# Keeping every softmax sum, testing their extremes at the end, and a second path on the chip for sums out of range

## The chip, the cores and the metric

The kernel runs on one core of one Trainium2 chip. The metric is the device time of one execution in microseconds (us). Before the change it is 411.09 us, the median of 3 runs (410.84 to 411.49).

The core has a matrix engine (PE, with its weight loads shown apart as PEld), three engines for elementwise work (DVE, ACT and POOL) and one that mostly issues transfers (SP). Each runs its own list of instructions in order, and they wait for each other through semaphores.

## The reference: what is computed

Two parts follow each other: a convolution whose seven taps have softmax weights of their own at every position and head, and a two-layer network with a maximum in the middle. Cut to what matters:

```python
# x: (8, 4160, 192), weight_gen: (8, 4160, 8 heads, 7 taps), w1 and w2: (192, 1024), w_out: (1024, 192), all float32
w = np.exp(weight_gen - np.max(weight_gen, axis=-1, keepdims=True))
w = w / (np.sum(w, axis=-1, keepdims=True) + 1e-09)
x_pad = concatenate([zeros((8, 6, 192)), x], axis=1)             # six rows of zeros ahead of each sequence
out = einsum('bshk,bskhg->bshg', w, x_unf)                        # x_unf[b, s, k] = x_pad[b, s + k], 8 heads of 24
h1, h2 = out @ w1, out @ w2
return np.maximum(h1, h2) @ w_out                                 # (33280, 192)
```

weight_gen is drawn with a standard deviation of 0.3 and x with 0.1.

## The kernel before

**The layout.** The 33,280 positions are dealt out to the 128 partitions: partition p holds 260 consecutive ones, called its columns. Columns go through in 17 batches, sixteen of 16 and one of 4; the batches are cut into units of 4 or 8 columns.

**The softmax without its maximum.** The kernel never subtracts the maximum. For a batch b, `exp_sum` (L135, ACT) takes the exponential of the loaded weights `wg_t` into `e_t`; `red` (L147, DVE) sums it over the seven taps into `sum_t`, a tile from a pool of three buffers; `ln` (L151, ACT) replaces the sum by its logarithm in place; `shift` (L156, DVE) subtracts that logarithm from the weights; and `weights` (L167, ACT) takes the exponential once more, now normalised, each value written twice in bfloat16 into `en_t`. This holds as long as the sums neither overflow nor vanish.

**The convolution and the network.** `mul` (L182, DVE) multiplies the taps into `m_t`, `adds` (L198, L204, L207, DVE) adds them up into `y_t`, and a transfer transposes the result into `yt` (L216, issued by SP; in the first two batches PE sums and transposes instead, L248). PE then forms h2 - h1 with the difference of the two weight matrices (`hid_tile`, L299), ACT takes its positive part (`relu`, L309) into `rd_t`, and PE adds `rd_t @ w_out` to `yt` times the product of w1 and w_out (`out_first`, L351, and `out_hidden`, L339). `evac` (L395, ACT) copies the result to `o_t`, and SP issues its store (L409). The last two columns have a tile of their own, `o_last` (copy L383); ACT and SP store one of them each (L386).

**The order** is written out by hand. Work is recorded in the order of the loop at the end (L785 to L800), engine by engine. `softmax_steps` and `extra` place the steps of later batches beside the matrix products of earlier groups of tiles, by the table `AT` and the dictionary `due`. After the last group, `rest_of_results` (L800) computes and stores the last results in three parts, and nothing but PE, ACT and the stores is left.

**The end.** The program closes with code that the framework puts in (recorded as L825, as L814 at the start): SP waits in turn for the semaphore of every transfer queue, then all engines meet in a barrier, POOL clears the semaphores, and they meet again.

Of the kernel before, what the change touches and what calls it, by code (L numbers as in the profile page):

```python
# [9 lines left out]
FP32 = mybir.dt.float32  # L10
BF16 = mybir.dt.bfloat16
# [6 lines left out]
def _sub(base: bass.AP, off: int, dims):  # L18
    ap = [list(base.ap[0])] + [[int(s), int(c)] for s, c in dims]
    return dataclasses.replace(base, offset=base.offset + off, ap=ap)  # L20
# [3 lines left out]
def kernel(  # L24
# [18 lines left out]
    HF = F // 2  # L43
    CPP = B * S // P
    RPB = P // B
    G = D // H
    assert RPB * CPP == S

# [24 lines left out]

    ctx.enter_context(tc.manual_schedule())
    consts = ctx.enter_context(tc.tile_pool(name="consts", bufs=1))
    pwg = ctx.enter_context(tc.tile_pool(name="pwg", bufs=4))
    pxb = ctx.enter_context(tc.tile_pool(name="pxb", bufs=2))
    pe_ = ctx.enter_context(tc.tile_pool(name="pe", bufs=2))
    psm = ctx.enter_context(tc.tile_pool(name="psm", bufs=3))
    pm = ctx.enter_context(tc.tile_pool(name="pm", bufs=1))  # L80
    pen = ctx.enter_context(tc.tile_pool(name="pen", bufs=2))
    py = ctx.enter_context(tc.tile_pool(name="py", bufs=2))
    pyt = ctx.enter_context(tc.tile_pool(name="pyt", bufs=6))
    prd = ctx.enter_context(tc.tile_pool(name="prd", bufs=7))
    first_ps = ctx.enter_context(ExitStack())
    ps = {k: first_ps.enter_context(tc.tile_pool(name="pps_" + k, bufs=2, space=bass.MemoryType.PSUM))
          for k in ("h", "o")}

    def later_ps():

        first_ps.close()
        for k in ("ab", "c", "r"):
            ps[k] = ctx.enter_context(tc.tile_pool(name="pps_" + k, bufs=1, space=bass.MemoryType.PSUM))

    wg_ts, xb_ts, e_ts, s_ts, en_ts, y_ts, yt_ts = {}, {}, {}, {}, {}, {}, {}

    m_t = pm.tile([P, K * 16 * D], BF16, name="m_t")

# [36 lines left out]
    def part(b, i, of):  # L137

        n = BATCHES[b][1]
        h0, h1 = n * i // of * H, n * (i + 1) // of * H  # L140
        return slice(h0, h1), h0 * K, [[K, h1 - h0], [1, K]]

    def red(b, i=0, of=1):
        if i == 0:
            s_ts[b] = psm.tile([P, BATCHES[b][1] * H], FP32, name="sum_t", tag="sum")
        hs, at, ap = part(b, i, of)
        nc.vector.reduce_sum(out=s_ts[b][:, hs], in_=_sub(e_ts[b], at, ap), axis=AX.X)  # L147

    def ln(b, i=0, of=1):
        s_t = s_ts[b][:, part(b, i, of)[0]]  # L150
        nc.scalar.activation(out=s_t, in_=s_t, func=AF.Ln)  # L151

    def shift(b, i=0, of=1):
        hs, at, ap = part(b, i, of)
        w_t = _sub(wg_ts[b], at, ap)
        nc.vector.tensor_tensor(out=w_t, in0=w_t, in1=_sub(s_ts[b], hs.start, [[1, hs.stop - hs.start], [0, K]]),  # L156
                                op=ALU.subtract)

    def weights(b, o):
# [293 lines left out]
    def out_room(now, tag=None):  # L453
        tag = tag or ("r" if "r" in ps else "o")
        w, name = {"ab": (2048, "ab"), "c": (1024, "c")}.get(tag, (1024, "op"))
        tile_ = ps[tag].tile([P, w], FP32, name="op_ps", tag=name)
        for c in now:
            op_at[c // 2] = tile_, (c - now[0]) // 2 * D
# [30 lines left out]
    def rest_of_results(c):  # L489

        parts = [p for p in (c[:4], c[4:-2], c[-2:]) if p]
        assert max(map(len, parts)) <= 4
        go = []
        for i, now in enumerate(parts):
            out_room(now, ("r", "ab", "c")[i])
            go.append(relay(out_first(now)))
            if i:
                out_second(parts[i - 1], go[i - 1])
                evac(parts[i - 1][0] // 2, len(parts[i - 1]) // 2)
        out_second(parts[-1], go[-1])  # L500
        evac(parts[-1][0] // 2, len(parts[-1]) // 2)
# [7 lines left out]
    msk_i = consts.tile([P, 1], I32, name="msk_i")  # L509
    msk = consts.tile([P, 1], FP32, name="msk")  # L510
    gate = consts.tile([P, 1], FP32, name="gate")
    o_last = consts.tile([P, 2 * D], FP32, name="o_last")

    with tc.tile_pool(name="pstage", bufs=1) as pstage:
# [179 lines left out]
        sum_transpose(3)  # L694
        weights(1, 8)

    pout = ctx.enter_context(tc.tile_pool(name="pout", bufs=1))
    o_t.append(pout.tile([P, 24 * D], FP32, name="o_t", tag="o"))


# [77 lines left out]
    def steps(g, tiles):  # L778

        if tiles:  # L780
            softmax_steps(g)
        for t in tiles:
            extra(t)

    out_room(OUTS[3])  # L785
    go = relay(out_first(OUTS[3]))
    out_second(OUTS[3], go)
# [2 lines left out]
    for g in range(4, len(GROUPS)):  # L790
        if GROUPS[g][1] == 3 and "c" not in ps:
            later_ps()
        tiles = [t for t in range(GROUPS[g][0], sum(GROUPS[g])) if t >= 16]
        if g in early:
            hidden(g, OUTS[g], early[g][0], ahead=lambda: {4: lambda: (weights(1, 12), ln(2)), }.get(g, none)())
            early[g][1]()
            steps(g, tiles)
        else:
            hidden(g, OUTS[g], beside=lambda: steps(g, tiles))
    rest_of_results(OUTS[-1])  # L800

# [1 line left out]
_INS = ['x', 'weight_gen', 'moe_w1', 'moe_w2', 'moe_w_out']  # L803
# [26 lines left out]
```

## Time and profile before

| what | value |
|---|---|
| median of 3 runs | 411.09 us (410.84 to 411.49) |
| the profiled execution: its own time | 411.11 us |
| the profiled execution: span, first to last instruction | 409.2 us |
| granted clock of PE | 1.000 |
| idle of ACT before L309, ended by PE | 26.2 us |
| DVE: reduces of the sums, L147 | 31 instructions, 19.6 us |
| ACT: logarithms of 128x128, L151 | 15 instructions, 5.0 us |
| SP: stores of o_t after 380 us, when issued | 384.20, 397.39, 399.93, 404.03, 405.27 us |
| the two stores of o_last, issue to landing | 1.8 us (SP) and 2.0 us (ACT) |

How to read it: the busy rows give each engine's busy time, its share of the span and its number of instructions; the slices cut the span in 40 equal parts, a digit for the busy share in tenths. A chain of work that ended last is followed back from the end: an engine with a large share of it sets the time. In a group of instructions the columns are line, engine, operation, output and input tile with their shapes and the count, then busy us and mean ns of one, then the idle time ahead of them and what ended it. "SPq" and "POOLq" are the sequencers of these engines: issues of transfers, waits and semaphore steps, which do not count as busy.

### The profile page before, as it was taken

The numbers are of one execution on the slowest core, as the hardware profiler recorded it, in microseconds if no ns is written. First come the engines' busy times: TensorE is split into PE (matmuls) and PEld (weight loads), VectorE is DVE, ScalarE is ACT, GpSimd is POOL, SyncE is SP. The second block draws the span as 40 slices with busy tenths as digits, with TensorE's granted clock in tenths as the row PEclk, the third lists the DMA queues.
The fourth block names the chain that finished last, engine by engine and source line by source line (L and its number), as shares of the span: only waits on it lengthen the run. The fifth ranks groups of instructions, "written<-read, shape, count | busy, mean of one in ns | idle before, by whom it ended". The sixth has DMA issues, their size and how long they took to land.

```text
span 409.2 us, 16135 instructions
## 1 busy us (share of the span) xinstructions
PE 399.1 (98%) x7422; PEld 317.7 (78%) x7422; DVE 371.9 (91%) x216; ACT 356.9 (87%) x424; POOL 74.3 (18%) x101
## 2 busy tenths in 40 slices
PE   7899899999999999999999999999999999999996
PEld 2589899777777877777787778777777877787796
DVE  5999999999999999899999999999999999999100
ACT  6799799999899998899998999998999888988872
POOL 0311120122222112122012222121122121210000
PEclk9999999999999999999999999999999999999999
DMA  8957657856658664964796496378649838743704
GB/s 239 228 128 214 115 155 161 184 144 165 148 113 243 155 155 108 239 151 96 151 249 157 94 263 172 76 230 210 122 91 258 168 51 221 186 88 89 205 34 163
DMA packets 60785, 65.70 MB, mean 161 GB/s; under 512 B 47631, under 2 KB 49039, under 8 KB 60718
## 3 DMA queue, kind: packets, MB, share of 16 engines
q1 hardware_dynamic: 52334, 40.54, 35.6%
q0 software_dynamic: 8240, 24.04, 29.6%
q8 instruction: 58, 0.95, 0.9%
q10 hardware_dynamic: 144, 0.10, 0.1%
q14 instruction: 9, 0.07, 0.1%
HBM read 35.96 MB, written 25.56 MB: 150 GB/s over the span
## 4 chain that ended last, share of the span: by engine, by line
PE 70%; DVE 18%; ACT 6%; DMA 3%; issue 2%; SPq 1%; DVEq 0%; ACTq 0%
PE op_ps L339 32%; PE hd L299 29%; DVE m_t L182 8%; PE op_ps L351 6%; DVE m_t L198 4%; DVE m_t L204 3%; ACT rd_t L309 3%; DMA ws1T<-in_moe_w_dram 2%; PE hdp L299 1%; PE yps L248 1%; DMA yt<-y_t 1%; DVE y_t L207 1%; DVE wg_t L156 1%; DVE sum_t L147 1%; ACT yt L255 1%
## 5 line engine op out<-in xcount | busy, mean ns | idle before, releaser
L309 ACT ACTIVATE rd_t<-hd 128x1024 bf16<-128x1024 f32 (+1 forms) x206 | 234.3, 1188 | 27.6 <-PE hd L299 26.2
L339 PE MATMUL op_ps<-wo,rd_t 64*128 64x192 bf16 x4160 | 211.7, 243 | 0.3 <-issue 0.2
L339 PEld LDWEIGHTS <-rd_t 64*128 64x128 bf16 x4160 | 181.8, 94 | 16.0 <-issue 0.4
L299 PE MATMUL hd<-yt,wd 64*128 64x512 bf16 (+1 forms) x1584 | 188.3, 360 | 0.4 <-DMA yt<-y_t 0.2
L182 DVE TENSOR_TENSOR m_t<-xb_t,en_t 128x10752 bf16<-128x10752 bf16 (+1 forms) x37 | 187.5, 5071 | 0.2
L299 PEld LDWEIGHTS <-wd 64*128 64x128 bf16 x1776 | 94.5, 94 | 42.4 <-issue 2.0
L224 POOL CAST gate<-yt 128x1 f32<-128x1 bf16 x29 | 39.4, 1358 | 270.0 <-DMA yt<-y_t 270.0
L198 DVE TENSOR_TENSOR m_t<-m_t 128x4608 bf16<-128x4608 bf16 (+1 forms) x30 | 74.1, 2471 | 0.1
L395 ACT COPY o_t<-op_ps 128x384 f32<-128x384 f32 (+1 forms) x99 | 57.2, 588 | 13.1 <-PE op_ps L339 13.1
L351 PE MATMUL op_ps<-w,yt 64*128 64x192 bf16 x780 | 56.0, 243 | 0.1
L351 PEld LDWEIGHTS <-yt 64*128 64x128 bf16 x780 | 38.7, 94 | 16.3 <-issue 0.9
L204 DVE TENSOR_TENSOR m_t<-m_t 128x3072 bf16<-128x3072 bf16 (+1 forms) x29 | 50.0, 1724 | 0.1
L167 ACT ACTIVATE en_t<-wg_t 128x896 bf16<-128x896 f32 (+2 forms) x45 | 35.8, 821 | 0.0
L207 DVE TENSOR_TENSOR y_t<-m_t 128x1536 bf16<-128x1536 bf16 (+1 forms) x29 | 27.3, 941 | 0.5
L156 DVE TENSOR_TENSOR wg_t<-wg_t,sum_t 128x280 f32<-128x280 f32 (+5 forms) x46 | 22.1, 482 | 2.3 <-ACT sum_t L151 2.3
L114 POOL DMA_DIRECT2D xb_t<-in_x_dram x33 | 17.6, 534 | 27.3 <-ACT rd_t L309 15.5
L147 DVE TENSOR_REDUCE sum_t<-e_t 128x64 f32<-128x448 f32 (+2 forms) x31 | 19.6, 636 | 2.8 <-ACT e_t L135 2.8
L135 ACT ACTIVATE e_t<-wg_t 128x896 f32<-128x896 f32 (+2 forms) x18 | 16.1, 900 | 2.8 <-DMA wg_t<-in_weight_gen_dram 2.8
L309 ACT ACTIVATE rd_t<-hdp 128x1024 bf16<-128x1024 f32 x16 | 16.2, 1054 | 0.4 <-PE hdp L299 0.4
L248 PE MATMUL yps<-ident,m_t 64*128 64x64 bf16 x636 | 11.0, 191 | 2.6 <-DVE m_t L182 1.6
L299 PE MATMUL hdp<-yt,wd 64*128 64x256 bf16 x192 | 13.1, 270 | 0.2
L248 PEld LDWEIGHTS <-m_t 64*128 64x128 bf16 x636 | 10.2, 95 | 3.9 <-DVE m_t L182 2.7
(45 smaller groups left out, 65.8 us busy)
## 6 DMA issues: line engine op xcount, KB each, us to landing
out_dram<-o_t SPq DMA_DIRECT2D x27, 768.0 KB, 4.7
xb_t<-in_x_dram POOLq DMA_DIRECT2D x30, 384.0 KB, 5.1
wg_t<-in_weight_gen_dram POOLq DMA_DIRECT2D x14, 448.0 KB, 5.5
xb_t<-xb_t POOLq DMA_DIRECT2D x16, 288.0 KB, 5.4
out_dram<-o_t SPq DMA_DIRECT2D x10, 384.0 KB, 2.9
wg_t<-in_weight_gen_dram SPq DMA_DIRECT2D x2, 448.0 KB, 4.6
xs<-in_x_dram SPq DMA_DIRECT2D x2, 384.0 KB, 6.7
xb_t<-in_x_dram POOLq DMA_DIRECT2D x3, 192.0 KB, 4.6
```

The source lines that it names most:

```text
L156: nc.vector.tensor_tensor(out=w_t, in0=w_t, in1=_sub(s_ts[b], hs.start, [[1, hs.stop - hs.start], [0, K]]), op=ALU.subtract)
L167: nc.scalar.activation(out=_sub(en_ts[b], (o * WGC + j * N * K) * 2, [[2 * N, K], [2, N], [1, 2]]), in_=_sub(wg_ts[b], (o * H + j * N) * K ...
L182: return nc.vector.tensor_tensor(out=m_out, in0=x_in, in1=_sub(en_ts[b], o * WGC * 2, [[2, K * n * H], [0, G // 2], [1, 2]]), op=ALU.mult,)
L198: nc.vector.tensor_tensor(out=taps(0, 1, 3), in0=taps(0, 1, 3), in1=taps(3, 1, 3), op=ALU.add)
L204: nc.vector.tensor_tensor(out=taps(0, 2, 2), in0=taps(0, 2, 2), in1=taps(1, 5, 2), op=ALU.add)
L207: nc.vector.tensor_tensor(out=_sub(y_ts[b], o * D, [[64, 2], [P, 3 * w // 2], [1, 64]]), in0=taps(0, 1, 1), in1=taps(2, 1, 1), op=ALU.add,)
L224: nc.gpsimd.tensor_copy(out=gate, in_=yt[:, 0:1])
L299: nc.tensor.matmul(hid_out(t, f, j), lhsT=wd_at(j, s, f // 4, f % 4 * P, P), rhs=_sub(yt_ts[u][half(j), :], (s + j) % 3 * P, [[3 * P, w // ...
L309: relu_of[t0] = nc.scalar.activation(out=rd[:, k * 1024:(k + n) * 1024], in_=hd[:, at:at + n * 1024], func=AF.Relu)
L339: return nc.tensor.matmul(op_out(c), lhsT=rd[half(r), k * 1024 + at:k * 1024 + at + P], rhs=wo[half(r), f * D:(f + 1) * D], start=False, s ...
L351: nc.tensor.matmul(op_out(c + j), lhsT=yt_ts[u][half(j), (3 * i + (s + j) % 3) * P:(3 * i + (s + j) % 3 + 1) * P], rhs=w10[half(j), s * D: ...
L395: nc.scalar.copy(out=_sub(o, c % 24 * D, [[D, len(qs)], [h * D, 2], [1, D]]), in_=_sub(tile_, at + (qs[0] - p) * D, [[D, len(qs)], [512, 2 ...
```

## The change

Four things are done.

1. The sums of the exponentials are no longer overwritten. `red` writes them into one of two tiles that live to the end, `sums[0]` (384 columns wide, for the first three batches) and `sums[1]` (1696 wide, for the rest); `ln` writes its logarithm into a tile `ln_t` from the pool that held `sum_t`, and `shift` reads that.
2. After the loop and ahead of `rest_of_results`, `out_of_range` is recorded: DVE takes the largest and the smallest of each of the two tiles per partition, compares them with 1e18 and 1e-18, and takes the maximum of the four answers. SP issues a transfer that turns the 128 answers, one per partition, into a row, and DVE takes its maximum as an integer `flag`, 0 or 1.
3. After `rest_of_results` all pools but `consts` are closed, every engine loads `flag` into a register and branches on it.
4. Where it is 1, `all_again` computes every column anew, one at a time in a loop of the chip, with the maximum subtracted, and overwrites all results. Where it is 0, the engines jump over it. On the path not taken the framework puts steps that bring the semaphores to where the second path would have left them: on SP eight, each a wait for a transfer queue's semaphore and an addition to it, and one each on PE, ACT and DVE. SP's closing waits are twelve in place of ten. SP's list also has four more register moves ahead of the first barrier.

```diff
+    S_MOST, S_LEAST = 1e18, 1e-18
...
-    wg_ts, xb_ts, e_ts, s_ts, en_ts, y_ts, yt_ts = {}, {}, {}, {}, {}, {}, {}
+    wg_ts, xb_ts, e_ts, l_ts, en_ts, y_ts, yt_ts = {}, {}, {}, {}, {}, {}, {}
+
+    sums = [consts.tile([P, 3 * 16 * H], FP32, name="sums")]
...
+    def s_of(b, hs):
+        c0 = BATCHES[b][0] * H - (b > 2) * 3 * 16 * H
+        return sums[b > 2][:, c0 + hs.start:c0 + hs.stop]
+
     def red(b, i=0, of=1):
-        if i == 0:
-            s_ts[b] = psm.tile([P, BATCHES[b][1] * H], FP32, name="sum_t", tag="sum")
         hs, at, ap = part(b, i, of)
-        nc.vector.reduce_sum(out=s_ts[b][:, hs], in_=_sub(e_ts[b], at, ap), axis=AX.X)
+        nc.vector.reduce_sum(out=s_of(b, hs), in_=_sub(e_ts[b], at, ap), axis=AX.X)
 
     def ln(b, i=0, of=1):
-        s_t = s_ts[b][:, part(b, i, of)[0]]
-        nc.scalar.activation(out=s_t, in_=s_t, func=AF.Ln)
+        if i == 0:
+            l_ts[b] = psm.tile([P, BATCHES[b][1] * H], FP32, name="ln_t", tag="ln")
+        hs = part(b, i, of)[0]
+        nc.scalar.activation(out=l_ts[b][:, hs], in_=s_of(b, hs), func=AF.Ln)
...
+    sums.append(pout.tile([P, (CPP - 3 * 16) * H], FP32, name="later_sums", tag="sums"))
...
+    def out_of_range():
+
+        for i, (op, beyond, limit) in enumerate(((ALU.max, ALU.is_gt, S_MOST), (ALU.min, ALU.is_lt, S_LEAST))):
+            for j in range(2):
+                nc.vector.tensor_reduce(out=ends[:, 2 * i + j:2 * i + j + 1], in_=sums[j], axis=AX.X, op=op)
+            nc.vector.tensor_single_scalar(out=ends[:, 2 * i:2 * i + 2], in_=ends[:, 2 * i:2 * i + 2],
+                                           scalar=limit, op=beyond)
+        nc.vector.tensor_reduce(out=bad, in_=ends, axis=AX.X, op=ALU.max)
+        nc.sync.dma_start(out=bad_row, in_=bad)
+        nc.vector.tensor_reduce(out=flag, in_=bad_row, axis=AX.X, op=ALU.max)
+
+    def all_again(pg, pgp):
...
+        for c0, c1 in ((0, PAD), (PAD, CPP)):
+            with tc.For_i(c0, c1) as c:
+                xw = pg.tile([P, K * D], FP32, name="g_xw", tag="g_xw")
+                nc.sync.dma_start(out=xw, in_=xe[:, bass.ds(c * D, K * D)] if c0 == 0
+                                  else x_rows[:, bass.ds(c - PAD, K), :])
+                a_column(xw, c)
...
+    out_of_range()
     rest_of_results(OUTS[-1])
+    fast.close()
+    any_bad = nc.values_load(flag[0:1, 0:1], min_val=0, max_val=1,
+                             skip_runtime_bounds_check_because="a maximum of comparisons, each 0 or 1")
+    with tc.If(any_bad > 0):
+        with tc.tile_pool(name="pg", bufs=1) as pg, tc.tile_pool(
+                name="pgp", bufs=1, space=bass.MemoryType.PSUM) as pgp:
+            all_again(pg, pgp)
```

In `all_again`, `a_column` loads one column's weights and x, computes its softmax with the maximum, multiplies and adds the taps on DVE, transposes on PE, runs the network and stores the column. The two tiles of sums shift the tiles that are allocated behind them to higher addresses.

## The prediction

> **What bounds the kernel now.** I read the span and clock of the core first (409.2 us, clock 1.000: nothing was throttled), then the page's busy rows and slices, then the chain of work that ended last, and then, because the change puts its new work at the end, the last 30 us one view at a time.
>
> ```profile
> PE 399.1 (98%) x7422; PEld 317.7 (78%) x7422; DVE 371.9 (91%) x216; ACT 356.9 (87%) x424; POOL 74.3 (18%) x101
> DVE   5999999999999999899999999999999999999100
> PE 70%; DVE 18%; ACT 6%; DMA 3%; issue 2%; SPq 1%; DVEq 0%; ACTq 0%
> ```
>
> PE is busy for 98% and carries 70% of the chain; DVE has 18% of it, all before the last three slices, where DVE stands idle. So work on DVE is dear up to about 380 us and free after it. The table of stretches says it sharply (columns: length, then PE, PEld, DVE, ACT and POOL with their counts, clock, DMA share, GB/s):
>
> ```profile
> 385.00:400.00 15.00, 15.00 (x314) 13.73 (x311) 0.00 (x0) 11.58 (x13) 0.00 (x0) 1.00 0.27 105
> 400.00:406.30 6.30, 5.34 (x130) 5.11 (x124) 0.00 (x0) 1.75 (x3) 0.00 (x0) 1.00 0.39 140
> 406.30:409.20 2.90, 0.00 (x0) 0.00 (x0) 0.00 (x0) 0.00 (x0) 0.00 (x0) 1.00 0.40 126
> ```
>
> The last 2.9 us hold no computing: only the last stores' landing and SP's closing waits. From the timelines, SP's waits and the records of L825 (the closing code):
>
> ```profile
> 379.49 0.56 DVE L207 TENSOR_TENSOR y_t<-m_t 128x768 bf16<-128x768 bf16 x1
> 405.88 0.34 SPq L386 DMA_DIRECT2D out_dram<-o_last  x1
> 405.89 0.37 ACTq L386 DMA_DIRECT2D out_dram<-o_last  x1
> SPq L825 <- DMA out_dram<-o_last: 0.6, 1, 0.6
> L825 SPq EVENT_SEMAPHORE  x7: 28/28/28, 407.9 to 408.3; - x7
> L825 POOLq EVENT_SEMAPHORE  x2: 17/17/17, 408.4 to 408.5; - x2
> ```
>
> The reader is to see the order of the end: DVE's last work ends at 380.05; the last two stores are issued until 406.22 (SP) and 406.26 (ACT); SP then waits for their landing until 407.92; from there to 408.34 it runs seven satisfied waits, one after the other, 0.42 / 7 = 61 ns each; then come the barriers, and the span ends at 409.2. POOL's two records are a wait that also takes from a semaphore and a plain add; narrowing the window puts them at 408.44 and 408.53, so a step that updates a semaphore costs about 80 ns.
>
> **What changes, step by step.** Read engine by engine, the two built programs have the same instructions with the same waits up to the end of DVE's, PE's and POOL's work, up to a semaphore's name on ACT, and on SP up to the store at 399.93. PE, ACT and DVE thus keep their order over 380 us. The durations below are of the profiled execution: 411.11 us, 1.9 more than its span, and 0.02 above the median of the three runs (411.09), so what I add to the one holds for the other.
>
> *Kept sums, Ln into a tile of its own.* 31 reduces (L147) and 18 logarithms (L151) keep their shapes; none is added. The tiles behind move up in memory by some KB. I take nothing: the multiplies of one form (L182, 128x10752) run in 5751 to 5756 ns on both turns of their buffers, so addresses do not show. Bounds: 0 to 0.1 us either way.
>
> *The test on DVE.* Two maxima and two minima over 384 and 1696 columns, two comparisons and one small maximum. From the reduces of before,
>
> ```profile
> L147 DVE TENSOR_REDUCE sum_t<-e_t 128x64 f32<-128x448 f32 x26 | 15.9, 613 | 2.8 <-ACT e_t L135 2.8
> L147 DVE TENSOR_REDUCE sum_t<-e_t 128x128 f32<-128x896 f32 x3 | 3.2, 1082 | 0.0
> ```
>
> 448 more elements cost 469 ns, 1.05 ns each, with 144 ns fixed: 0.55 us for 384, 1.92 for 1696, together 2 x 2.47 = 4.9, and three small ones at 0.15 (L560) = 0.5. From 380.05 DVE is done at 385.4. It is beside PE and ACT, and its first reader is SP's DMA, which stands behind the store of 399.93: 14.9 us of cover. Were the cover gone, it would cost 5.4.
>
> *The DMA of one number per partition into a row, and its maximum.* SP issues it at 400.33, for some 0.4 (as its neighbours). Behind it on SP stands the store at 404.03: 3.3 us to spare. It lands after 1.8 us (o_last) to 5.4 (the slowest of the last five o_t stores, 2.0/3.0/5.4), so at 402.1 to 405.7; DVE's maximum (0.15) gives the flag by 402.3 to 405.9, ahead of SP's and ACT's first need for it at 406.22 and 406.26. Cost 0.
>
> *The load of the flag and the branch, on each engine.* DVE and POOL do it as soon as the flag is there, PE after 405.35, ACT and SP after 406.22. On SP and ACT it lies beside the landing, which ends at 407.92: 1.66 us of cover. The trace has no register load. Its ends are 17 ns (an SP semaphore record) and 1.8 us (a whole store of 96 KB, issue to landing); one word out of SBUF is a round trip, but a shorter one than that store's, so I take 1.0, nearer to the upper row. The branch: SP's gap from its last issue (406.22) to the first closing record (406.27) holds a branch already and is 0.05. 406.22 + 1.0 + 0.05 = 407.3, covered. [...]
>
> *What SP does on the path not taken.* Here is the cost that nothing hides. The not-taken path raises eight DMA semaphores by what the second path would have raised them, each raise waiting for its own DMAs; SP's closing waits are twelve instead of ten, and all of them come behind the raises. Before, seven records stood behind the last landing. Now there are six raises (the first two pass while the landing runs), a branch, and twelve waits: 6 x 0.08 + 0.05 + 12 x 0.061 = 1.26, against 7 x 0.061 = 0.43. The barriers behind are unchanged. **Sum: +0.83 us, 411.11 + 0.83 = 411.9.** Bounds of this step: raises and waits at 0.05 (the spacing of SP's first two closing records, 53 ns) give 0.95 - 0.43 = +0.5; all at 0.08, with 0.1 of branch, +1.1.
>
> *At the start* SP sets four registers more before the first barrier. Its first record is at 0.00 and POOL's constants hold that barrier to 0.5, so four at 0.06 are hidden.
>
> **Rivals.**
>
> 1. *The closing steps are cheap* (not slower). All of it hangs on the mean price of a step: 18 new and old steps and the branch must exceed 0.43 + 0.82, so the side is decided at (1.25 - 0.05) / 18 = 67 ns a step. For cheap: SP's own records stand 53 and 61 ns apart. Against: none of those updates a semaphore, and POOL's that do stand 80 apart. At 53 ns: +0.5, 411.6, within 0.2%.
>
> 2. *The load outlasts the landing.* It decides from 1.6 us on. For: five engines fetch the same word, and a round trip through memory takes 1.8 here. Against: it is one word. At 1.8 to 2.2 SP enters the path at 408.1 to 408.5, with all eight raises ahead: 8 x 0.08 + 0.05 + 0.73 = 1.42, drain at 409.5 to 409.9 against 408.34: +1.2 to +1.6, **412.3 to 412.7**.
>
> 3. *The jump leaves the fetched code.*
>
> ```profile
> q8 instruction: 58, 0.95, 0.9%
> q14 instruction: 9, 0.07, 0.1%
> ```
>
> (queue, packets, MB, share of 16 engines.) 0.95 MB over PE's 14,844 instructions is 64 bytes each, in packets of 16 KB (256 instructions); the other engines share 9 of 8 KB (about 120). The second path lies between the branch and its target: 209 instructions on PE, 99 on SP, 91 on DVE, 66 on ACT, 52 on POOL. Each is under a packet, so the target is in the packet being run or in the next one. PE runs through its 58 packets with 0.3 us of idle time before L339 in all, so the next one is fetched ahead. That speaks against a stall. If jumps did refetch: 0.1% of 16 x 409.2 us over 9 is 0.7 us a packet, and 1.8 for the round trip, 2.5; SP then enters at 409.8, and with 1.42 behind drains at 411.2: +2.9, **413 to 414.5**. [...]
>
> 4. *The change does not do what it says*, and the second path runs: sums of seven exponentials of inputs of deviation 0.3 lie near 7, far from 1e18 and 1e-18. Under 1 in 100; it would add 260 columns, one after the other, behind the end.
>
> **How the numbers follow.** A difference under 0.2% (0.82 us) can't be told from none here, and my sum lies on that bound. Forecast, 411.6 to 412.2: 55%, of it 30 above the bound (411.91) and 25 below. Rival 1: 13%, below. Rival 2: 17%, above. Rival 3 with 4: 12%, above. Faster, by a luckier landing of the last stores: 3%. Slower 30 + 17 + 12 = 59%, same 25 + 13 = 38%, faster 3%. The range, 411.4 to 412.9, takes in forecast and rivals 1 and 2 (85%) and leaves out rival 3 and the gain.
>
> **What would show it.** Right: the spans from 0 to 405.9 us agree to 0.1; DVE's test ends before 387; the DMA of the row lands before 405.9; SP's raises begin before 407.9; from the last landing to SP's drain 1.1 to 1.4 us instead of 0.43. Wrong: a load of over 1.6 us, or a hole between the branch and the first raise, with a new packet in the instruction queues; or the stores of 404.03 and after later than before.

## The result, and the profile after

The changed kernel takes 414.02 us (median of 7 runs, 412.42 to 415.40) against 411.09 for the kernel before beside it (7 runs, 410.14 to 412.31): a ratio of 1.0074, 95% interval 1.0056 to 1.0092. That is +3 us where +0.8 was forecast, outside the range. The profiled execution took 413.74 us, span 411.9, clock 0.999; before, 411.11 and 409.2. Verdicts below are ratios to the kernel before, run on the same chip (its medians there: 410.9, 411.29, 410.71 and 410.73 us in the four sets). They leave out executions more than 1.5% above the fastest of their kernel, which were found in e8 alone. The lines of the changed kernel shown here count 8 higher than before, and the closing code is L926 instead of L825.

The timeline of the changed kernel at its end (start, length, engine, line; in brackets the idle time before and what ended it):

```profile
385.31 0.16 DVE L805 TENSOR_REDUCE bad<-ends 128x1 f32<-128x4 f32 x1
...
403.77 0.27 DVE L807 TENSOR_REDUCE flag<-bad_row 1x1 int32<-1x128 f32 x1 [18.30 <-DMA bad_row<-bad]
...
406.45 0.35 SPq L394 DMA_DIRECT2D out_dram<-o_last  x1
406.45 0.38 ACTq L394 DMA_DIRECT2D out_dram<-o_last  x1
```

The test is done at 385.47 and the flag at 404.04, both ahead of need. The last stores are issued 0.57 us later than before (406.45 against 405.88). Now the table of stretches, cut where PE, ACT and DVE are all done (columns as in the prediction):

```profile
400.00:406.90 6.90, 5.91 (x144) 5.68 (x138) 0.27 (x1) 2.23 (x5) 0.00 (x0) 1.00 0.45 164
406.90:411.90 5.00, 0.00 (x0) 0.00 (x0) 0.00 (x0) 0.00 (x0) 0.00 (x0) 0.87 0.26 78
```

The part without computing has grown from 2.9 to 5.0 us. What fills it is told by SP's waits, by the records of SP in the branch's line L898 (its semaphore raises) and in L926, narrowed to the stretch behind the last landing, and by POOL's drain (count, then least, median and longest in ns, then first and last start in us):

```profile
SPq L898 <- SPq L898: 2.3, 3, 1.3
L898 SPq EVENT_SEMAPHORE  x6: 17/17/17, 409.8 to 410.2; - x6
L926 SPq EVENT_SEMAPHORE  x12: 28/28/28, 410.2 to 410.9; - x12
L926 POOLq DRAIN  x3: 46/107/5436, 405.1 to 411.6; - x3
```

SP sits in three raises that wait for stores, 1.3 us in the longest; six raises stand behind the last landing (409.798 to 410.22, 70 ns each) and then twelve waits (62 ns each, drain at 410.966). POOL's drain of 5.4 us, which ran from 384.30 to 389.89 before, starts at 405.11 now and ends at 410.55, 0.42 us ahead of SP's. The transfers in that stretch (queue, packets, MB, share; then KB and us from issue to landing), with the two rows of the page that count instruction packets in the whole run below them:

```profile
q14 instruction: 3, 0.02, 1.7%
q8 instruction: 1, 0.02, 1.7%
...
out_dram<-o_t SPq DMA_DIRECT2D x1, 192.0 KB, 2.7
out_dram<-o_last SPq DMA_DIRECT2D x1, 96.0 KB, 3.1
out_dram<-o_last ACTq DMA_DIRECT2D x1, 96.0 KB, 3.3
```

```profile
q8 instruction: 59, 0.97, 0.9%
q14 instruction: 12, 0.10, 0.1%
```

Here is what the forecast did not have: four packets of instructions more than before (58 and 9), all in the last microseconds (8 KB at 406.27, 406.82 and 408.52, PE's 16 KB at 407.52), and the last stores land after 3.1 and 3.3 us instead of 1.8 and 2.0.

For this one execution the sum closes: stores issued 0.57 later, landing 1.31 longer (3.33 against 2.01), SP's part behind the last landing 0.74 longer (1.17 against 0.43), together 2.62 of the 2.63 us. The last two of these terms belong to the end; the first came about ahead of it and is taken up below.

The landing records tell more. A store lands in 16 shares. Before, all sixteen of ACT's came 1.85 to 2.01 us after issue. After the change thirteen come at 1.80 to 1.99, and three at 2.24, 2.70 and 3.33; of SP's store thirteen by 1.82, and three at 2.41, 2.54 and 3.13. Each store is held up by a few late shares.

### The profile page after: what moved, and what is told of

It is laid out like the page before. It is cut to its first block, busy times and chain, and to the rows that moved or that the text cites. A ratio compares the mean times of both kernels' runs of the same rounds, so it can differ in the third digit from the quotient of the medians.

```text
span 411.9 us, 16172 instructions
## 1 busy us (share of the span) xinstructions
PE 399.6 (97%) x7422; PEld 317.6 (77%) x7422; DVE 377.2 (92%) x224; ACT 356.9 (87%) x424; POOL 73.9 (18%) x101
## 4 chain that ended last, share of the span: by engine, by line
PE 69%; DVE 18%; ACT 6%; DMA 3%; issue 2%; SPq 1%; DVEq 0%; ACTq 0%
PE op_ps L347 32%; PE hd L307 29%; DVE m_t L190 8%; PE op_ps L359 6%; DVE m_t L206 4%; DVE m_t L212 3%; ACT rd_t L317 3%; DMA ws1T<-in_moe_w_dram 2%; PE hdp L307 1%; DMA yt<-y_t 1%; PE yps L256 1%; DVE y_t L215 1%; DVE wg_t L164 1%; DVE later_sums L153 1%; ACT yt L263 1%
## 5 line engine op out<-in xcount | busy, mean ns | idle before, releaser
L164 DVE TENSOR_TENSOR wg_t<-wg_t,ln_t 128x280 f32<-128x280 f32 (+5 forms) x46 | 22.0, 480 | 2.6 <-ACT ln_t L159 2.6
L153 DVE TENSOR_REDUCE later_sums<-e_t 128x64 f32<-128x448 f32 (+2 forms) x27 | 16.2, 600 | 0.3 <-ACT e_t L139 0.3
L627 PE MATMUL warm<-ident 128*128 128x512 bf16 x38 | 11.1, 461 | 2.7 <-DVE ident L574 2.7
```

The lines of the kernel that those rows point to most:

```text
L164: nc.vector.tensor_tensor(out=w_t, in0=w_t, in1=_sub(l_ts[b], hs.start, [[1, hs.stop - hs.start], [0, K]]), op=ALU.subtract)
```

## The experiments

**Theory F:** a jump over the second path takes an engine into a new block of its instructions, a block is fetched at that, and the packet delays the share of a store that goes the same way. Rivals: **B**, loads and taken branches cost it by themselves; **L**, the row's transfer and the register loads crowd the end; **C**, the kept sums and the test slow the body. The length of a block is an estimate: the packets of q8 have 16,384 bytes each and those of q14 8,192 (59 and 12 of them in the changed kernel), which at the 64 bytes of an instruction that the prediction works out is 256 instructions for PE and 128 for the other engines; one packet is taken as one block. From this, the built programs and the places of packets in the body the place of each block's edge in an engine's list was estimated, to within a few instructions.

The table sums up all profiles: T is the time from the issue of the last stores to the end of the span, which leaves out what happened ahead of it. A share counts as late at over 2.1 us (without a packet near the stores none came later than 2.05; in e9, whose packets lie further off, 2.09). Packets are given by their start, relative to the issue, from 1.6 us ahead of it on. (e8 has a start of its own and is left out.)

```
run                         packets near the last stores        late shares SP/ACT   last landing after    T
before                      none                                0 / 0                2.01                  3.3
changed                     -0.17 +0.37 +1.07(16 KB) +2.07      3 / 3                3.33                  5.4
e1_test_only                none                                0 / 0                2.05                  3.3
e2_load_no_branch           none                                0 / 0                2.04                  3.9
e3_no_pe_path               -0.47 -0.38 +2.33                   2 / 2                2.80                  4.9
e4_no_pe_path_sp_pad        +0.39 +0.45 +2.08                   2 / 2                2.97                  5.2
e5_one_loop                 +0.41 +0.46 +2.09                   2 / 2                2.96                  6.8
e6_one_loop_pads            +0.31 +0.89                         2 / 2                2.53                  6.4
e7_one_loop_pool_pads       +0.38 +1.69                         1 / 2                2.65                  7.1
e9_row_on_act               -1.59 -1.48 +1.72(16 KB) +2.09      0 / 0                2.09                  4.2
e10_pads                    +3.69                               0 / 0                2.05                  4.7
e11_pads_row_on_act         +3.84                               0 / 0                2.05                  4.5
e12_fetch_no_branch         +0.31 +2.48                         1 / 1                2.47                  3.7
e13_tiny_path               none                                0 / 0                2.05                  4.2
e14_tiny_path_row_on_pool   none                                0 / 0                2.01                  3.3
e15_row_on_pool             +1.05(16 KB) +2.08                  1 / 1                4.01                  6.2
e16_all_mended              none                                0 / 0                2.03                  3.4
```

**First set: parts of the change.**

```diff
e1: after out_of_range() and rest_of_results: no load, no branch, no second path
-    any_bad = nc.values_load(...)
-    with tc.If(any_bad > 0): ...
e2: the load alone, its value unused
-    with tc.If(any_bad > 0): ...
e3: in a_column, the second path without PE
-            tp = pgp.tile(...)   # and all matmuls down to op
e4: e3, and at the start
+        for i in range(6): nc.sync.dma_start(out=spare[0:1, i:i + 1], in_=...)
```

> Left out: the load of the flag, the branch and the second path; the kept sums, the test, the transfer of the row and the integer flag stay. Theory F (the jumps enter new blocks of instructions, PE's and SP's, and those fetches sit on transfer engines that carry shares of the last stores): no extra instruction packet (58 and 9), the o_last stores land 1.8 to 2.0 us after issue, seven closing waits behind the last landing, +0.0 to +0.2 us against before (ratio 1.000). Rival L (the row transfer and the register loads crowd the end): the row's part of it would still be here, landing over 2.5, +0.5 to +1. Rival C (the kept sums slow the body by the 0.6 seen in the one profile): o_last issued at 406.4 instead of 405.9, +0.6.

Measured 1.0004 (0.9989 to 1.002), which is 0.2 us, with no packet near the end and the last landing after 2.05 us. L falls as far as it meant the row's transfer. C's 0.6 us becomes unlikely, but the interval reaches 0.8, so it is not excluded.

> Left out: the branch and the second path; each engine still loads the flag into a register. F: 58 and 9 instruction packets, landing 1.8 to 2.1, the load of 0.5 us hidden beside it, some closing waits more: +0.1 to +0.4 us. L: loads of five engines delay the stores, landing over 2.8 as in the changed kernel, +1.3 to +2. C: +0.6, as for the test alone.

1.0018 (1.0006 to 1.0029). The unused load was dropped in the build and only the waits for the flag stayed, so it doesn't test the load. It left a hint that I read only later: POOL's drain ran from 402.85 to 408.22 and SP's stood at 407.62, so POOL was the last.

> The branch and the two loops stay; left out of the second path: all of its matrix products and what feeds them, so that its result would not be the reference's (it does not run on these inputs). PE's jump is 49 instructions instead of 209 and ends in the block that PE runs in; the others' jumps stay. F: 58 packets of 16 KB instead of 59, 12 of 8 KB as before, no packet near 407.5 but SP's near 408.5; PE's compare and branch takes under 0.1 us instead of 1.0; the o_last stores land after 2.0 to 2.6 instead of 3.1 to 3.3; time +0.8 to +1.6. Rival B (any taken branch costs this, whatever its length): landing over 3, +2.9 as the changed kernel.

1.0056 (1.0036 to 1.0075), with PE's packet gone and one late share of each store less. The sizes missed F's expectation: the landings of 2.4 and 2.8 us lie partly above its 2.0 to 2.6, the time is 2.3 us over instead of 0.8 to 1.6, and PE's branch took 0.24 us instead of under 0.1.

> As the kernel without PE in the second path, and six transfers of one word each are added to SP's list early, while it stands idle, so that SP's branch and its target both lie in its third block and no fetch of SP follows the jump. F: no instruction packet between 407 and SP's closing waits; landing 1.8 to 2.1; what is left is the tail of raises and waits, +0.75 (last landing to SP's drain 1.15 instead of 0.43): time +0.7 to +0.9. B: landing over 3, +2.9. If SP's fetch does nothing, the same as without the six transfers.

1.0057 (1.0035 to 1.008). The padding was too short, SP still crossed the edge, and the run says nothing of SP.

**Second set: jumps made short, edges padded away.**

```diff
e5: one loop over x staged in bfloat16 in place of two loops
-        for c0, c1 in ((0, PAD), (PAD, CPP)): ...
+            nc.gpsimd.dma_start(out=xa[:, (PAD + q) * D:(PAD + q + 65) * D], in_=...)
+        with tc.For_i(0, CPP) as c: ...
e6: e5, and 30 transfers on SP at the start, and behind out_of_range()
+    for _ in range(38): nc.vector.memset(pad_v, 0.0)
+    for _ in range(36): nc.gpsimd.memset(pad_p, 0.0)
e7: e6 with the second path's transfers on POOL (nc.gpsimd), 34 transfers on SP, 32 memsets on POOL
e8: before, its PE list longer at the start
-        keep_warm(30)
+        keep_warm(15)
+        for _ in range(79): nc.tensor.matmul(warm[:, 0:64], lhsT=ident, rhs=ident[:, 0:64], ...)
```

> The second path as one loop over bfloat16 columns (it computes the same, with x rounded to bfloat16), so that PE jumps over about 107 instructions instead of 209 and stays in its block of 256, and ACT stays in its own; SP, DVE and POOL still jump into a new block of 128. Theory F (a jump into a new block of instructions fetches it, and the fetch delays the last stores on the transfer engines): 58 packets on the first instruction queue and 12 on the second, no 1010 ns branch on PE, the two last stores land 2.3 to 2.9 us after their issue, the time 0.45 to 0.65% over the kernel before. Theory B (every taken branch costs it, whatever it jumps over): 59 packets, landings of 3.1 to 3.3 us, 0.7% over. Theory L (the flag's loads cost it): as the changed kernel, 0.7%.

1.0088 (1.0072 to 1.0103). PE's packet is gone and two shares are late, as F says, but the time rose. The transfers that POOL issues in the second path have to be accounted for on the path not taken (1.49 us on POOL), and its drain behind that ended at 413.77, 2.7 us after SP's.

> The same, and as many small instructions ahead of the branch on SP (30 transfers of 4 bytes at the start), DVE (38 memsets) and POOL (36 memsets) as bring branch and target into one block of 128: no engine jumps into a new block. F: no instruction packet is fetched in the last 2 us, the last stores land 1.8 to 2.1 us after their issue as before, and only the closing steps stay (+0.7 to +0.8 us): 0.15 to 0.25% over the kernel before. B and L: landings of 2.5 to 3.3 us and 0.5 to 0.75% over, since loads and branches are all there.

1.0083 (1.007 to 1.0096). The expectation failed: the padding moved the edges into the last microseconds instead of away from them (SP's came with its last instructions, DVE's among the memsets, which also delayed DVE's branch to 409.07). Two packets, two late shares; POOL's drain was last again.

> As the run above, and the second path's transfers issued by POOL instead of SP, so that POOL, which is idle, raises the semaphores on the path not taken, and SP has only its closing waits. F with closing steps of 61 ns: landings of 1.8 to 2.1 us, 0.3 to 0.5 us from the last landing to SP's drain more than before at most, 0.05 to 0.15% over the kernel before. If the raises on POOL wait for the landing as SP's did, the drain of POOL takes the place of SP's: 0.2%. B and L: 0.4% or more.

1.0101 (1.0077 to 1.0124), failed in the same way, POOL's drain ending at 412.31.

> The kernel before, without any branch, with 128 more small instructions on PE in its warm-up (15 matmuls of it in 79 narrow ones), so that PE's last block of 256 begins with the last products and is fetched while the last stores run. F (it is the fetch, not the branch): the last packet of the first instruction queue starts after 404 us and the last stores land 0.3 to 1.0 us later than the 1.8 to 2.0 us of the kernel before; time 0.05 to 0.25% over, apart from what the warm-up itself changes (the first real product's start is compared). B: landings of 1.8 to 2.0 us, no change. If the next block is fetched well ahead, the packet lies before 404 us and nothing is told.

1.0006 (0.9961 to 1.005), from four of its twelve executions, and nothing told: the packet came at 406.69, 4.95 us ahead of the last stores, and over before them. The narrow warm-up also made the runs uneven (409.5 to 420.5).

**Third set: edges padded away with room, and a fetch without a branch.**

```diff
e9: the changed kernel, the row issued by ACT
-        nc.sync.dma_start(out=bad_row, in_=bad)
+        nc.scalar.dma_start(out=bad_row, in_=bad)
e10: e3, 40 transfers on SP at the start, and around the test
+    for _ in range(45): nc.vector.memset(pad_v, 0.0)
     out_of_range()
+    for _ in range(40): nc.gpsimd.memset(pad_p, 0.0)
e11: e10 with e9's edit
e12: e1, 33 transfers on SP at the start, 5 memsets on DVE ahead of the test and 28 behind it
```

> The changed kernel with one edit: ACT issues the DMA of the row instead of SP, at the place in ACT's order that stands before its last two evictions, so the flag should be there by 387 to 396 us instead of 403.8, and POOL and DVE jump early. Two things in the changed kernel stand behind the flag and near the end: POOL's closing drain of 5.4 us (405.1 to 410.5, before it ran from 384.3 to 389.9) and the fetches of POOL's and DVE's new blocks (406.3 and 406.8). Theory F (the fetches delay the last stores): two of the four late packets move to before 400 us, PE's (about 407.5) and SP's (about 408.5) stay, so one share of each last store instead of three is late, by about 0.6 to 1.3 us; POOL's drain ends before 403; 0.3 to 0.8 us less than the changed kernel, 0.45 to 0.65% over the kernel before. Theory B or L (branches or loads by themselves, or the row's landing): landings of 3.1 to 3.3 us stay, time within 0.2 us of the changed kernel.

1.0059 (1.0039 to 1.0078). ACT took the row up only at 400.41, so the flag came at 403.9 and not by 396: that part of the expectation failed. But the packets of POOL and DVE happened to lie 1.5 us ahead of the stores, PE's and SP's behind 1.7, and no share was late. The last stores' issue was 1.29 us later in this profile; 0.73 of it stood at 12 us already, long before the edit acts, and most of the rest came at about 55 us and after 320. POOL's drain ended at 410.36, not before 403. So the 0.59% lies in the range that was expected, but it came about another way.

> The second path without its matrix products (left out there; it does not run), so that PE stays in its block, and 40, 45 and 40 small instructions on SP (at the start), DVE (ahead of the test) and POOL (behind its last cast), so that each branch and its target lie in one block of 128. F: no instruction packet after 404.9 us, the last stores land within 1.8 to 2.1 us of their issue, SP's part behind the last landing is 1.1 to 1.2 us, and SP's drain is 0.7 to 0.8 us later than in the kernel before, measured from the issue of the last store. But POOL's drain still starts behind the flag at about 404.5 and lasts 5.4 us, so it would now end last, at about 409.9: 0.3 to 0.45% over the kernel before. B or L: landings of 2.4 us or more, as in the run without matrix products and without padding (0.56%).

1.0056 (1.0032 to 1.008), above the 0.3 to 0.45% expected. Of the transfers between 405.4 and 408.6 the profile says:

```profile
q1 hardware_dynamic: 688, 0.69, 63.0%
q10 hardware_dynamic: 144, 0.10, 9.7%
```

There is no instruction packet, and no share is late, with all loads and branches in place: B and L fall for the landing. Yet the time did not follow, for two reasons that the end shows. (The end explains 1.4 of the 2.3 us by T; the rest lies ahead of the last stores.) POOL's drain went to 410.36 and SP's came at 410.15, so POOL was last, as expected. And SP itself was 0.4 us later than it should be: between two of its closing waits, 0.06 to 0.09 apart otherwise, lie 0.38 us, and 0.6 us later a packet is fetched. By the count this is where the padding pushed SP's next edge, so running over an edge may have stopped SP itself; the trace shows the hole, not its cause.

> The same and ACT issues the DMA of the row, so that POOL's drain is done before 403 us. F: all that is left are SP's closing steps, 0.7 to 0.8 us: 0.15 to 0.25% over the kernel before, and the profile ends with SP's waits again. If POOL's drain was not what ended last in the run above, no difference from it.

1.0047 (1.003 to 1.0063), twice what was expected. POOL's drain was over at 408.85 (not before 403, since ACT again took the row up late, at 399.4) and SP was last again, at 409.83. From the last issue to SP's drain it takes 1.20 us more than before: the 0.7 to 0.8 expected, and the hole, which is there too (0.38 us). Of the rest of the 1.9 us the profile shows 0.28 ahead of the last stores; some 0.4 it does not show.

> No load, no branch, no second path (left out): only the test, and small instructions on SP (33 transfers at the start) and DVE (5 memsets ahead of the test, 28 behind the flag) that put the crossing into a new block of 128 on SP and on DVE into the last microseconds, by running straight on. The run with the test alone showed 1.0004, landings of 1.8 to 2.1 us and no late packet. F: two packets of 8 KB at about 406.2 to 407.4 us, two shares of each of the two last stores 0.5 to 0.9 us behind the other fourteen, the end 0.5 to 0.9 us later: 0.1 to 0.25% over the kernel before. B (it is the branch): landings of 1.8 to 2.1 us, no difference. A fetch that comes after 407.9 us tells nothing.

1.0024 (1.0007 to 1.0042). There is no load, branch or second path here. The edges of two engines were moved to the end, one packet came in time, and one share of each store is late:

```profile
q14 instruction: 1, 0.01, 0.7%
```

(from 405 to 407.7 us; the second packet started at 407.75, too late to matter.) The last share came at 2.47 us instead of 2.05. So here a store was late beside a packet without any branch. By T this is 0.4 of the 1.0 us that the ratio says.

**Fourth set: what is left.** POOL's drain was by now a theory of its own, **P**: it is a second limit, 0.42 us behind the first in the changed kernel. **D** is that the body in front of the last stores is slower by itself with a branch in the kernel.

```diff
e13: the changed kernel with a tiny second path
-            all_again(pg, pgp)
+            o = pg.tile([P, D], FP32, name="g_o", tag="g_o")
+            nc.vector.memset(o, 0.0)
+            nc.sync.dma_start(out=..., in_=o)
e14: e13, and
-        nc.sync.dma_start(out=bad_row, in_=bad)
+        nc.gpsimd.dma_start(out=bad_row, in_=bad)
e15: the changed kernel with e14's row
e16: e15, the second path as one loop over x staged in device memory (pool pgd), all its
     transfers on SP; 50 transfers on SP at the start, 45 memsets on DVE, 40 on POOL as in e10
```

> Test, row, five loads and five branches as in the changed kernel, but in place of the second path one memset and one store (the recomputation is left out; the path does not run), so that each branch jumps over a few instructions and stays in its block. Theory F (fetches of new blocks): no instruction packet in the last 2 us, landings of 1.8 to 2.1 us; theory B (loads and branches by themselves): landings of 2.4 us or more. Theory P (POOL's closing drain, 5.4 us, starts only behind POOL's branch): POOL's drain ends about 1.2 us behind SP's, and the profile ends 1.2 to 1.6 us later than in the kernel before, counted from the issue of the last store: 0.3 to 0.45% over. Without P: 0.05 to 0.1% (a raise or two more on SP).

> The same and POOL issues the DMA of the row, right when the test is done, so that POOL loads the flag by about 388 to 392 us and its drain is over by 400. P: the end goes back to SP's waits, 0.1 to 0.4 us behind the kernel before: 0.02 to 0.15% over. Without P: no difference from the run above. If the body in front of the last stores is slower by itself with a branch in the kernel (theory D, some 0.5 us were seen in the profiles, of which chance may be all), 0.15 to 0.25% stays.

1.0043 (1.0023 to 1.0064) and 1.0019 (1.0 to 1.0039). The drains of e13 (behind x3 the three drains of an engine: the long one is POOL's first, and SP's first is where its waits are done):

```profile
L927 POOLq DRAIN  x3: 46/107/5372, 404.8 to 410.7; - x3
L927 SPq DRAIN  x3: 7/7/13, 409.2 to 410.5; - x3
```

and of e14:

```profile
L927 POOLq DRAIN  x3: 46/107/5454, 389.9 to 408.3; - x3
L927 SPq DRAIN  x3: 7/7/13, 407.7 to 408.0; - x3
```

In e13 SP is done at 409.21 and the barrier waits until 410.24 for POOL, whose drain ends at 410.19. With the flag there at 389 instead of 404, POOL's drain ends at 395.4, and the barrier follows SP by 0.1 us. P stands, with 0.9 us (T is 4.2 against 3.3). And with five loads and five branches, but short jumps, e14's time from the last issue to SP's drain is 2.463 us against 2.465 before: loads and branches cost nothing at the end. But e14's ratio, 0.8 us over, is more than P expected (0.02 to 0.15%) and lies in what D expected (0.15 to 0.25%); its profile shows none of it, and the interval reaches down to none. D stays open.

> The changed kernel with one edit: POOL issues the DMA of the row. POOL's and DVE's branches and their packets move to about 388 to 394 us, POOL's drain ends by 400; PE's packet (about 407.5) and SP's (about 408.5) stay. F: one share of each of the two last stores late instead of three, by about 0.6 to 1.3 us; 0.2 to 0.6 us less than the changed kernel, 0.55 to 0.7% over the kernel before. B: as the changed kernel, 0.7%.

1.0068 (1.0042 to 1.0094). Three of the steps came as expected (packets of POOL and DVE at 391.6 and 391.8, POOL's drain over at 396.5, one late share), and the size did not. Transfers from 405.7 to 409.8:

```profile
q8 instruction: 1, 0.02, 2.1%
q14 instruction: 1, 0.01, 0.8%
...
out_dram<-o_last SPq DMA_DIRECT2D x1, 96.0 KB, 3.8
out_dram<-o_last ACTq DMA_DIRECT2D x1, 96.0 KB, 4.0
```

One share of each store was held back by 2.0 us, more than in the changed kernel with its four packets. PE's packet of 16 KB ran from 406.80 to 408.18, SP's of 8 KB from 407.82 to 408.31. Here are the transfers from 407.45 to 408.16 us:

```profile
q14 instruction: 1, 0.01, 4.3%
```

and from 408.16 to 409.1:

```profile
q1 hardware_dynamic: 9, 0.01, 3.4%
q10 hardware_dynamic: 9, 0.01, 3.4%
```

While PE's packet ran on, nothing of the two stores moved. All 18 packets of the two late shares follow, the first at 408.17, when PE's packet ended: the share stood behind the fetch. It then moved slowly as well, at 64 to 111 ns a packet up to 408.8 and 36 after that, so a part of the 2.0 us may be SP's fetch. Two packets fewer brought nothing, because a store lands with its last share (ACT's here at 4.01 us).

> Everything of the changed kernel computed, with all three found causes taken out that can be: the second path as one loop over x staged in device memory (PE jumps over 107 instructions and stays in its block of 256), small instructions ahead of the branch on SP (50 transfers at the start), DVE (45 memsets ahead of the test) and POOL (40 memsets), so that each branch and its target lie in one block of 128, and the DMA of the row issued by POOL. F and P: no packet in the last 2 us, landings of 1.8 to 2.1 us, POOL's drain over by 400 us, SP's part behind the last landing 1.1 to 1.2 us: 0.7 to 0.8 us of closing steps are left, 0.15 to 0.25% over the kernel before; with D 0.3 to 0.4%. If it stays at 0.55% or more, F and P do not carry the time.

1.0000 (0.9974 to 1.0026). The medians are 411.38 against 410.73 us (0.16% apart), both with a wide spread here. From 405.5 to 408.7 us, and at the end:

```profile
q1 hardware_dynamic: 688, 0.69, 63.5%
q10 hardware_dynamic: 144, 0.10, 9.9%
```

```profile
L934 POOLq DRAIN  x3: 46/107/5454, 399.3 to 409.7; - x3
L934 SPq DRAIN  x3: 7/7/13, 409.1 to 409.4; - x3
```

No packet near the end, no late share, POOL done at 404.7 (not by 400, but early enough). The closing steps vanished as well, which I had not expected: in this build no raise waits for the last two stores, so all raises run while those land, and from the last issue to SP's drain it takes 2.50 us against 2.47. T is 3.4 against 3.3, from 5.4 in the changed kernel: the end is back to what it was, with the packets, POOL's drain and, by luck, the closing steps out of the way. D is not settled by it: the stores were issued 0.71 us later than before in this profile, the medians differ by 0.65 us, and the ratio's interval allows 1.1. No version beat the kernel before; e16 does the whole of the change at a cost that can't be told from none, within 0.26%.

## Why the prediction was wrong

Of the 3.0 us, 2.1 stand behind the issue of the last stores (T): 0.74 are SP's closing steps, which the forecast had, and 1.31 the longer landing, which it did not. The other 0.9 lie ahead of the last stores, and their cause is open. Point by point, in the prediction's order:

- **The kept sums and the test: right.** Reduces of 0.55 and 1.91 us, done at 385.47 (forecast 385.4); e1 prices them with the row's transfer at 1.0004.
- **The row: right.** It landed after 2.8 us, in time; cost 0 at its place. That it comes late matters for POOL, below.
- **Load and branch: right that they are covered, the load too dear.** 0.49 to 0.54 us in the five loads of the changed kernel instead of 1.0, so rival 2, which needed 1.6, is out. The branch took 45 to 72 ns on four engines (forecast 50).
- **SP's closing steps: right in size.** +0.74 measured, +0.83 forecast; raises 70 ns, waits 62. Rival 1's 53 ns did not come. What the sum did not say is that it hangs on which semaphore a raise waits for: e16 has the same kinds of steps, at +0.03.
- **The landing of the last stores, taken as it was: this step failed, by 1.31 us.** The forecast kept the landing's end (407.92) fixed, and put packets of instructions only against the engine that jumps, never against the stores. The runs showed that the stores land later with such packets near: after 3.33 us with four of them, 2.47 with one and no branch (e12), 2.05 with all branches and none near (e10, e13).
- **Rival 3 named the right cause with the wrong mechanism.** It said that with a target "in the packet being run or in the next one", and the next one fetched ahead, there is no stall, and gave 12%, together with rival 4, for a refetch that stalls SP for 2.5 us. SP did not stall: its branch took 58 ns, and its first raise waited for a store. The author's reading, which no run shows by itself, is that the next block is fetched ahead and entering it calls for the one behind it. The trace fits that: POOL, DVE, PE and SP each ran on behind their branch (405.11, 405.3, 406.5 and 408.2) before the packets started (406.27, 406.82, 407.52, 408.52), so these did not bring what the engines were running. By the count four engines entered a new block at the end, and it was the stores that came later, by 1.31 us. The measured 414.02 lies in that rival's 413 to 414.5, but not by its stall. What the count of 209, 99, 91, 66 and 52 jumped instructions should have been held against is not the length of a packet but where the edges lie: by that count only ACT's jump stayed inside its block.
- **POOL's drain was not looked at.** The forecast said nothing of moving it from 384.3 to 405.1. Hidden by 0.42 us in the changed kernel, it is the end in e13 (+0.9), e10, e2, and e5 to e7. Even with no packet the forecast would have been short: without the 1.31 us SP would have been done at 409.65 in this profile, and POOL still at 410.55 (an estimate from these figures).
- **"The spans from 0 to 405.9 agree to 0.1": this failed too, and the cause is open.** The last stores are 0.57 later here, in jumps of some 0.25 at about 55 and 320 us. Between 80 and 320 us the changed kernel and the one before keep their distance to within 0.04 us, so the kept sums cost nothing there. Over all profiles the issue of the last stores lies between 405.2 and 407.8 (405.2 to 405.9 in the four without a branch, 405.2 to 407.8 in the thirteen with one, e8 aside). What the ratio says beyond T is 0.9 us in the changed kernel and 0.6 on average over the kernels with a branch, about 0 in e15 and e16, and 0.3 in the three without. The two groups differ too little and too unevenly to name D the cause, and the record does not settle how much is chance. What the start-up does to it was not tried.

From the distances of the targets the prediction took that a jump into the packet being run or into the next one does not stall. On POOL, SP and DVE the branch agrees with that: 45, 58 and 72 ns, by the count with a new block (changed kernel) or without (e10). On PE it does not: its branch took 231 to 236 ns inside a block (e10, e3, e11) and 1010, 1290 and 1574 ns into the next one (changed kernel, e15, e9); nothing waited for it. What the prediction left out is that such a packet can run beside the last stores: with packets near, shares landed 0.2 us (the changed kernel's earliest late one, 2.24) to 2.0 us (e15, 4.01) late.

That a packet and the late share use the same one of the 16 transfer engines is argued, from the counts (a store has 16 shares, and packets that start between 0.5 us before the issue and 1.7 behind it agree with the late shares in the table, but for one of SP's in e7) and from the order in e15; the trace does not name the engine of a packet. Why a packet of 0.31 us can hold a share back by up to 1.0 is not shown.

## What to carry to other kernels

Here five loads and five branches at the end of the kernel cost nothing there by themselves (e14, with short jumps: 2.463 us from the last issue to SP's drain, 2.465 before); what came with the jump over cold code did. By the count four engines landed in a new block of their lists, four packets of instructions ran around the last stores, and a store, as late as its latest share, landed after 3.33 us instead of 2.01. Look where the edges lie (packets of the instruction queues in the last microseconds tell it), keep cold code short or pad the edges away (2.05 us in e10, 2.03 in e16; a wrong count moves them into the end, as in e6 and e7, 2.53 and 2.65), and make what the branch waits for ready early, because an engine's closing drain stands behind its branch (POOL's started at 404.8 us in e13, where the flag came at 404, and at 389.9 in e14, where it came at 389). And in pricing a tail, ask of each engine what it used to do unseen, not only of the one that ended last.

## What the runs showed of the hardware

- With a packet of 8 KB (0.31 to 0.38 us long in the changed kernel) that started between 0.5 us before the issue of a 96 KB store and 1.7 after, one of the store's 16 shares landed 0.2 to 1.0 us late (e3 to e7, e12 and the changed kernel, whose latest share, 1.3 late, had PE's 16 KB near as well; in e7 SP's store has one late share for two packets). With PE's 16 KB (1.38 us), and 8 KB of SP's beside its end, one landed 2.0 late (e15).
- POOL's first drain at the end took 5.4 to 5.6 us in every profile (5.37 in e10 and e13, 5.44 in the changed kernel, 5.59 before), whether it started at 384 us (before) or at 408 (e5).
- SP stopped for 0.38 us among its closing waits, 0.06 to 0.09 apart otherwise, where by the count it runs straight over an edge (e10, e11).
- The same transfer of one number per partition into a row landed after 2.4 to 3.4 us from SP (eleven profiles; 2.8 in the changed kernel), 3.0 and 3.2 from ACT (e11, e9) and 3.5, 4.1 and 1.9 from POOL (e14, e15, e16). The moment differs too, so the engine need not be the cause.
- A register load of a word of on-chip memory took 0.49 to 0.54 us (the five loads of the changed kernel); a semaphore wait on SP 62 ns, one that also raises 70 (changed kernel).
